# Taking GpSimd's arithmetic out of a fused attention and two-MoE kernel

## The chip, the cores and the metric

The kernel runs on one core of a Trainium2 chip. A core has four compute engines that run side by side: TensorE (PE, the matrix engine), VectorE (DVE), ScalarE (ACT) and GpSimd (POOL). A fifth, SyncE (SP), issues most of the DMAs. The metric is the device time of one execution in microseconds, the median of several runs.

## The reference, cut to what matters

```python
scores = scale * q @ k^T                      # 2 batches, 12 heads, 448 x 448, head size 64
scores = where(upper triangle, -1e9, scores)
attn = exp(scores - max(scores)); attn = attn / (sum(attn) + 1e-9)
x = attn @ v                                  # reshaped to 896 tokens x 768
a = x @ w1; b = x @ w2                        # 768 x 1024 each
y = (a * b @ w3) @ w_out                      # 1024 x 1024, 1024 x 768
h = y @ w_in; g = max(h, 0) ** 2              # 768 x 2048
out = g @ w_out2                              # 2048 x 768
```

## The kernel before, in words

The kernel keeps float32 accuracy on TensorE by splitting each operand into two parts: a rounded one ("hi", fp32r) and the remainder ("lo"). A product is then three fast matmuls: hi x hi, hi x lo and lo x hi. ScalarE makes hi by a rounding copy, and VectorE makes lo by the subtraction x - hi. `parts_of` (L442) records these two steps. Large products use Strassen's scheme with seven products per 2 x 2 block, which needs sums and differences of blocks. Most of these are VectorE's too.

The work has three stages. In the first (until about 158 us of the profile), the 12 pairs of heads go through attention, and TensorE's gaps are filled with the product of w3 and w_out (tiles `w`). `scores` (L620) makes two heads' score blocks, `minimum` adds the mask and takes the row extreme on VectorE, `softmax` (L666) has ScalarE's exponentials, VectorE's reciprocals, and then one division (a multiplication by the reciprocal, L689) per block of 112 rows, eight per pair. `transposes` and `attend` follow on TensorE. The second stage computes a, b and their product with the combined weight matrix. The third (from about 312 us) has four groups of the second MoE: for each, `product` makes h, `g_out` (L1004) applies ReLU and the square on ScalarE, `need_block` (L1020) makes the Strassen blocks of g (sums in `fs`, parts in `g`), and `o_step` multiplies them with w_out2, whose parts lie in `ring`. `into_acc` (L1187) adds the results from PSUM into tiles named `g`. Weights come by DMA into `raw` tiles, are put together in `xs`, and are split into `ring`.

The order of the instructions is worked out while the kernel is built, by `Program` (L26). Each `prog.add(engines, run, reads, writes, ...)` records an operation with its cost on each engine that may run it: "T" TensorE, "A" ScalarE, "V" VectorE, "P" GpSimd, "S" DMA. `order` (L60) gives every operation a due time from the TensorE operations that need it, then simulates the engines greedily: at each step the engine that can begin earliest takes the ready operation with the earliest due time. TensorE's operations keep the order in which the program lists them. The order that comes out is the order of each engine's instructions on the chip, where semaphores keep the dependences.

Three things of this planner belong to GpSimd. An operation marked `port=True` (both operands in SBUF) on VectorE can't begin in the plan while one on GpSimd is running, nor the other way round. An operation that VectorE could also run goes to GpSimd only if it would end there before VectorE could begin to come to it, or if it is due more than `SPARE` = 2500 ns later. And 64 operations end up on GpSimd: 27 of the 96 divisions of the softmax, and 37 subtractions, which are parts and differences of blocks of h and g. Beside that GpSimd builds two constants at the start and issues the 12 accumulating DMAs of `w_sums` (L810).

The divisions' and subtractions' alternatives are recorded like this:

```python
        engines = dve(width) | (pool(width) if any_engine else {})
        prog.add(engines, tt(lo, x, lambda: hi().bitcast(F32), ALU.subtract), src + his, los, port=not psum)
```

All two-operand instructions of VectorE and GpSimd recorded through `tt` have line L433 in the profile; ScalarE's copies have L440.

Of the kernel before, what the change touches and what calls it, by code (L numbers as in the profile page):

```python
# [16 lines left out]
class Op:  # L17
# [4 lines left out]
    def __init__(self, place, engines, run, after, behind, port):  # L22
        self.place, self.engines, self.run, self.port = place, engines, run, port
        self.after, self.behind = after, behind
        self.due = self.start = self.end = None


class Program:
# [4 lines left out]
    SPARE = 2500  # L33
# [4 lines left out]
    def add(self, engines, run, reads=(), writes=(), port=False, after=(), behind=(), turn=None):  # L38
# [11 lines left out]
        op = Op(len(self.ops), engines, run, list(after), [o for o in behind if o not in after], port)  # L50
        if turn:
            self.turns[turn] = op
        for r in reads:
            self.read.setdefault(r, []).append(op)
        for r in writes:
            self.wrote[r], self.read[r] = op, []
        self.ops.append(op)
        return op

    def order(self):  # L60
# [68 lines left out]
def attention_moe_moe2(ctx: ExitStack, tc: tile.TileContext, qk, v, w1, w2, w3, w_out, w_in2, w_out2, out):  # L129
# [210 lines left out]
    engine_of = {"A": nc.scalar, "V": nc.vector, "P": nc.gpsimd}  # L340
# [8 lines left out]

    def pool(width):  # L350
        gap = 110 + 2.28 * width
        return {"P": (gap, gap + 30)}
# [89 lines left out]
    def parts_of(hi, lo, x, width, src, his, los, psum=False, any_engine=False, of=None):  # L442
# [6 lines left out]
    def block_parts(of, n, k, x, src, psum=False, any_engine=False):  # L449
        slot = slot_of_block(of, n, k)  # L450
        parts_of(lambda: part_of_slot(slot, 0), lambda: part_of_slot(slot, 1), x, S, src,
                 part_names(slot, 0), part_names(slot, 1), psum, any_engine, of)
# [29 lines left out]
    def float32(key, words, width, y, names):  # L482
# [16 lines left out]
        prog.add(dve(width, fast=True), lower, [low], [low], port=True)  # L499
        prog.add(dve(width), join, [low, *names], names, port=True)  # L500
# [14 lines left out]
    def w_row(key):  # L515
# [26 lines left out]
        prog.add(dve(width), tt(lo, y, lambda: hi_of(key).bitcast(F32), ALU.subtract), src + his, los, port=True)  # L542
# [77 lines left out]
    def scores(p):  # L620
# [9 lines left out]
        for g in BLOCKS:  # L630
            o = 0
            for i in g:
# [13 lines left out]
                prog.add({"T": (1.856 * w, 1.856 * w + 250)}, run, [("qk", p % 3)],  # L646
# [19 lines left out]
    def softmax(p, j):  # L666
# [169 lines left out]
    for k in range(KH):  # L836
        i, b = slot_in("T2", k), slot_in("B21", k)
        prog.add(dve(S), tt(fs_at(i), fs_at(b), fs_at(i), ALU.subtract), [("fs", i), ("fs", b)], [("fs", i)], port=True)
# [14 lines left out]
    def half_sum(out, x, z, what):  # L853
# [5 lines left out]
        prog.add(dve(HN), tt(half(out), half(x), half(z), what), [xs_half(*x), xs_half(*z)], [xs_half(*out)], port=True)  # L859
# [32 lines left out]
    def need_unit(u):  # L892
# [25 lines left out]
        else:  # L918
# [5 lines left out]
                 src + [("ring", i, "h") for i in slots], [("ring", i, "l") for i in slots], port=True)  # L924
# [19 lines left out]
    def ab_out(nm, m, b, n, i_bank):  # L944
# [12 lines left out]
        else:  # L957
            prog.add(dve(S), negated(row, fs_at(n), fs_at(a), ALU.mult), [("fs", n), ("fs", a)], names, port=True)
# [21 lines left out]
    def ab_sums(d):  # L980

        (r0, n0), (r1, n1), (r2, n2), (r3, n3) = (ab_row(d, i) for i in range(4))
        prog.add(dve(S), tt(r0, r0, r1, ALU.subtract), n0 + n1, n0, port=True)
        prog.add(dve(S), tt(r1, r3, r1, ALU.subtract), n1 + n3, n1, port=True)

        def t2():
            t = take_fs()
            prog.add(dve(S), negated(fs_at(t), r3, r0, ALU.subtract), n3 + n0, [("fs", t)], port=True)
            block_parts("ab", "T2", d, fs_at(t), ("fs", t))
            prog.add(dve(S), negated(r2, r2, fs_at(t), ALU.subtract), [*n2, ("fs", t)], n2, port=True)  # L990
# [13 lines left out]
    def g_out(nm, m, b, n, i):  # L1004
# [10 lines left out]
        parts_of(*part, lambda: fs[:, n, BN:], REST, ("fs", n), his, los, any_engine=True)  # L1015
# [4 lines left out]
    def need_block(g, n, d):  # L1020
# [7 lines left out]
        def sub(out, x, y):  # L1028
            prog.add(dve(BN) | pool(BN), tt(fs_at(out, BN), fs_at(x, BN), fs_at(y, BN), ALU.subtract),
                     [("fs", x), ("fs", y)], [("fs", out)], port=True)  # L1030
# [6 lines left out]
        elif n == "7":  # L1037
# [3 lines left out]
                 his, los, any_engine=True)  # L1041
# [101 lines left out]
    def h_out(n, k, st, i):  # L1143
        o, src = bank_at(i), ("bank", i)

        def block(name, at):
            block_parts("h", name, k, fs_at(at), ("fs", at), any_engine=True)
# [4 lines left out]
        def sub(out, x, y):  # L1152
            prog.add(dve(S), tt(fs_at(out), fs_at(x), fs_at(y), ALU.subtract), [("fs", x), ("fs", y)], [("fs", out)],
                     port=True)
# [183 lines left out]
```

## Time and profile before

| | us |
|---|---|
| median of 3 runs | 534.0 |
| lowest and highest | 533.85 and 537.04 |
| the profiled execution | 534.52 |
| its span, first to last instruction | 532.7 |

The profile comes from that one execution. It gives each engine's busy time, groups of equal instructions with their mean duration, the instructions in order of time, and the chain of waits followed back from the last instruction. Instructions of one engine overlap at their ends, so n in a row take less than n times the duration of one.

### The profile page before, as it was taken

The numbers are of one execution on the slowest core, as the hardware profiler recorded it, in microseconds if no ns is written. First come the engines' busy times: TensorE is split into PE (matmuls) and PEld (weight loads), VectorE is DVE, ScalarE is ACT, GpSimd is POOL, SyncE is SP. The second block draws the span as 40 slices with busy tenths as digits, with TensorE's granted clock in tenths as the row PEclk, the third lists the DMA queues.
The fourth block names the chain that finished last, engine by engine and source line by source line (L and its number), as shares of the span: only waits on it lengthen the run. The fifth ranks groups of instructions, "written<-read, shape, count | busy, mean of one in ns | idle before, by whom it ended". The sixth has DMA issues, their size and how long they took to land.

```text
span 532.7 us, 8568 instructions
## 1 busy us (share of the span) xinstructions
PE 519.2 (97%) x2905; PEld 460.8 (86%) x2905; DVE 492.3 (92%) x1093; ACT 383.9 (72%) x890; POOL 103.2 (19%) x84
## 2 busy tenths in 40 slices
PE   7899999999999999999999999999999999999996
PEld 4658878888879999999999999999999989998985
DVE  5999898898999999997975899999999999999996
ACT  6998887777869565648475577986896489649950
POOL 2222211122110010221100034010115021505050
PEclk9999999999999999999999999999999999999999
DMA  8956554452642469999652402405430454035114
GB/s 317 322 166 220 169 180 148 147 170 61 249 156 83 177 184 252 260 254 248 153 163 93 172 0 73 165 1 201 155 120 0 148 178 150 0 132 175 51 59 149
DMA packets 26572, 81.30 MB, mean 153 GB/s; under 512 B 2400, under 2 KB 13408, under 8 KB 26528
## 3 DMA queue, kind: packets, MB, share of 16 engines
q1 hardware_dynamic: 22752, 75.24, 41.4%
q0 software_dynamic: 3776, 5.51, 6.4%
q8 instruction: 23, 0.38, 0.3%
q14 instruction: 21, 0.17, 0.1%
HBM read 74.84 MB, written 14.55 MB: 168 GB/s over the span
## 4 chain that ended last, share of the span: by engine, by line
PE 54%; DVE 21%; ACT 7%; DMA 2%; issue 2%; DVEq 0%
PE bank L176 43%; DVE g L433 6%; DVE ring L433 5%; PE w L176 5%; DVE xs L433 2%; DVE xs L495 2%; PE pp L704 2%; PE x L176 2%; DVE fs L433 2%; PE s L176 2%; ACT ring L440 1%; DMA raw_w<-in_w 1%; DMA raw_wout<-in_w_out 1%; ACT fs L1010 1%; ACT fs L1011 1%
## 5 line engine op out<-in xcount | busy, mean ns | idle before, releaser
L440 ACT CAST ring<-xs 128x384 fp32r<-128x384 f32 (+1 forms) x194 | 102.3, 542 | 59.2 <-DVE xs L433 21.4
L176 PE MATMUL bank<-xT,ring 128*128 128x448 f32 x630 | 132.2, 366 | 0.0
L433 DVE TENSOR_TENSOR ring<-xs,ring 128x384 fp32r<-128x384 f32 (+1 forms) x194 | 118.9, 631 | 12.2 <-ACT ring L440 12.0
L176 PEld LDWEIGHTS bank<-xT,ring 128*128 128x128 f32 x630 | 117.8, 188 | 9.6 <-ACT bank L440 0.5
L176 PE MATMUL bank<-ring,g 128*128 128x384 f32 x600 | 107.7, 337 | 3.0 <-DVE ring L433 2.0
L176 PEld LDWEIGHTS bank<-ring,g 128*128 128x128 f32 x600 | 103.8, 188 | 6.5 <-DVE ring L433 3.3
L176 PE MATMUL bank<-xB,ring 128*128 128x448 f32 x489 | 103.5, 367 | 0.7 <-ACT ring L440 0.4
L176 PEld LDWEIGHTS bank<-xB,ring 128*128 128x128 f32 x489 | 91.3, 188 | 10.0 <-ACT ring L440 1.4
L433 POOL TENSOR_TENSOR g<-fs,g 128x384 fp32r<-128x384 f32 (+1 forms) x24 | 37.2, 1562 | 127.7 <-ACT g L440 112.5
L672 ACT ACTIVATE p<-p,st 112x448 f32<-112x448 f32 (+3 forms) x96 | 49.9, 533 | 12.1 <-DVE st L662 12.1
L689 POOL TENSOR_SCALAR p<-p,st 112x224 f32<-112x224 f32 (+3 forms) x27 | 33.5, 1244 | 114.3 <-DVE st L681 62.4
L433 DVE TENSOR_TENSOR xs<-xs 128x384 f32<-128x384 f32 x96 | 54.4, 581 | 0.1
L662 DVE CUSTOM_DVE_ANT_0 p<-s,mask 112x224 f32<-112x224 f32 (+3 forms) x96 | 36.7, 440 | 6.4 <-PE s L176 6.3
L440 ACT CAST g<-fs 128x384 fp32r<-128x384 f32 (+1 forms) x88 | 34.4, 413 | 5.2 <-DVE fs L433 4.9
L176 PE MATMUL w<-hl_wout,w 128*128 128x384 f32 x192 | 36.2, 340 | 0.3 <-DVE wraw L433 0.2
L487 ACT ACTIVATE xs<-raw_w 128x768 f32<-128x768 f32 (+1 forms) x30 | 24.3, 814 | 14.7 <-DVE w L433 6.5
L176 PEld LDWEIGHTS w<-hl_wout,w 128*128 128x128 f32 x192 | 32.9, 188 | 1.9 <-issue 0.9
L821 POOL DMA_DIRECT2D s_dram<-w_dram x12 | 13.9, 1184 | 99.6 <-DMA s_dram<-w_dram 99.6
L176 PE MATMUL s<-qk 64*112 64x448 f32 (+3 forms) x192 | 28.2, 439 | 3.9 <-DMA qk<-in_qk 3.9
L433 DVE TENSOR_TENSOR g<-bank,g 128x384 f32<-128x384 f32 x60 | 30.1, 544 | 1.6 <-PE bank L176 1.6
L440 ACT COPY fs<-bank 128x448 f32<-128x448 f32 x49 | 25.8, 527 | 7.6 <-PE bank L176 7.6
L176 PE MATMUL bank<-ab,ring 128*128 128x448 f32 x144 | 29.5, 365 | 0.0
(82 smaller groups left out, 746.7 us busy)
## 6 DMA issues: line engine op xcount, KB each, us to landing
raw_wout<-in_w_out SPq DMA_DIRECT2D x24, 768.0 KB, 4.5
raw_w<-in_w SPq DMA_DIRECT2D x16, 768.0 KB, 4.5
raw_win<-in_w_in SPq DMA_DIRECT2D x16, 768.0 KB, 4.5
raw_w<-in_w SPq DMA_DIRECT2D x16, 512.0 KB, 4.1
qk<-in_qk SPq DMA_DIRECT2D x12, 448.0 KB, 5.7
s_dram<-w_dram POOLq DMA_DIRECT2D x8, 576.0 KB, 9.8
w_dram<-wraw SPq DMA_DIRECT2D x8, 384.0 KB, 2.9
s_dram<-w_dram SPq DMA_DIRECT2D x4, 768.0 KB, 7.1
```

Source lines behind the costliest of these rows:

```text
L176: return nc.tensor.matmul(o, l, r, start=start, stop=stop, **more)
L433: return lambda e: engine_of[e].tensor_tensor(out(), x(), y(), op=what)
L440: return lambda e: engine_of[e].copy(out(), x()) if e == "A" else engine_of[e].tensor_copy(out(), x())
L487: nc.scalar.activation(y(), raws[key][:, :, 1].bitcast(F32), AF.Prelu, scale=2.0 ** -112, alpha=-2.0 ** 32)
L495: nc.vector.scalar_tensor_tensor(yi, yi, 3, raws.pop(key)[:, :, 0], op0=ALU.logical_shift_left, op1=ALU.bitwise_or)
L662: prog.add({"V": (gap, gap + 160)}, lambda e: nc.vector.tensor_tensor_reduce(block(p, j, i), s_t[p, j, g][:CP, o:o + w], mask[:, S - w:], ...
L672: prog.add({"A": (gap, gap + 100)}, lambda e, i=i: nc.scalar.activation(block(p, j, i), block(p, j, i), AF.Exp, bias=st_t[p][:, 0, j, i:i ...
L689: lambda e, i=i: engine_of[e].tensor_scalar(block(p, j, i), block(p, j, i), st_t[p][:, 3, j, i:i + 1], None, ALU.mult),
L704: nc.tensor.transpose(x[0][:CP, o * CP:(o + 1) * CP], block(p, j, i)[:, c * CP:(c + 1) * CP], ident[:CP, :CP])
L821: prog.add({"P": (900, 5000)}, lambda e, x=x, n0=n0, n1=n1: nc.gpsimd.dma_start(out=s_dram[d][:, n0:n1], in_=spread(x, n1 - n0), accum_op= ...
L1010: prog.add(act(S, src[0] == "bank"), lambda e: nc.scalar.activation(r(), x(), AF.Relu), [src], [("fs", n)])
L1011: prog.add(act(S), lambda e: nc.scalar.activation(r(), r(), AF.Square), [("fs", n)], [("fs", n)])
```

## The change

No operation has GpSimd as an alternative any more: the divisions are VectorE's alone, and so are all subtractions. With that, the planner loses its rule for the shared port (the `port` marks and the time that the port is held) and the rule with `SPARE`. One cost of the plan changes too: the scores of the first pair of heads (p == 0) are planned at 3.3 ns per column in place of 1.856. The DMA issues of `w_sums` and the two constants stay with GpSimd.

```diff
-    SPARE = 2500
...
-        port, at_step = 0, 0
+        at_step = 0
...
                 def begin(o):
-                    held = port if e in "PV" and o.port else 0
-                    return max(clock[e], avail[o], held)
+                    return max(clock[e], avail[o])
...
-                if e in "AP":
+                if e == "A":
...
-                        return t0 + o.engines[e][0] < on_v or e == "P" and o.due > t0 + self.SPARE
+                        return t0 + o.engines[e][0] < on_v
...
-            if e in "PV" and o.port:
-                port = t0 + gap
...
-    engine_of = {"A": nc.scalar, "V": nc.vector, "P": nc.gpsimd}
+    engine_of = {"A": nc.scalar, "V": nc.vector}
...
-    def pool(width):
-        gap = 110 + 2.28 * width
-        return {"P": (gap, gap + 30)}
...
-        engines = dve(width) | (pool(width) if any_engine else {})
-        prog.add(engines, tt(lo, x, lambda: hi().bitcast(F32), ALU.subtract), src + his, los, port=not psum)
+        prog.add(dve(width), tt(lo, x, lambda: hi().bitcast(F32), ALU.subtract), src + his, los)
...
-                prog.add({"T": (1.856 * w, 1.856 * w + 250)}, run, [("qk", p % 3)],
+                prog.add({"T": ((3.3 if p == 0 else 1.856) * w, (3.3 if p == 0 else 1.856) * w + 250)}, run, [("qk", p % 3)],
...
-                on_v, on_p = 70 + 0.67 * w, 265 + 2.5 * w
-                prog.add({"V": (on_v, on_v + 85), "P": (on_p, on_p + 30)},
-                         lambda e, i=i: engine_of[e].tensor_scalar(
+                on_v = 70 + 0.67 * w
+                prog.add({"V": (on_v, on_v + 85)},
+                         lambda e, i=i: nc.vector.tensor_scalar(
...
-            prog.add(dve(BN) | pool(BN), tt(fs_at(out, BN), fs_at(x, BN), fs_at(y, BN), ALU.subtract),
-                     [("fs", x), ("fs", y)], [("fs", out)], port=True)
+            prog.add(dve(BN), tt(fs_at(out, BN), fs_at(x, BN), fs_at(y, BN), ALU.subtract),
+                     [("fs", x), ("fs", y)], [("fs", out)])
```

## Rows read from the trace of the kernel before

**Rows 1.** The page: busy us, share of the span, instructions of each engine.
```profile
PE 519.2 (97%) x2905; PEld 460.8 (86%) x2905; DVE 492.3 (92%) x1093; ACT 383.9 (72%) x890; POOL 103.2 (19%) x84
```
**Rows 2.** Stretches of the span: PE, PEld, DVE, ACT, POOL busy us, clock, DMA.
```profile
0.00:158.00 158.00, 152.01 (x1020) 118.55 (x1022) 142.00 (x440) 124.28 (x344) 35.14 (x35) 1.00 0.57 194
...
378.00:479.00 101.00, 99.11 (x527) 93.10 (x526) 100.29 (x194) 72.97 (x164) 23.14 (x18) 1.00 0.33 111
479.00:505.00 26.00, 25.83 (x130) 23.68 (x131) 25.81 (x56) 24.46 (x58) 7.24 (x1) 1.00 0.35 119
505.00:523.00 18.00, 16.39 (x89) 14.90 (x87) 18.00 (x31) 9.00 (x21) 8.17 (x7) 1.00 0.14 44
```
**Rows 3.** The chain that ended last, in order of time: start, us, what.
```profile
158.75 184.03 PE bank L176 x911
...
511.18 1.29 DVE fs L433
```
**Rows 4.** TensorE: two undisturbed runs by time; then its groups, 378.6 to 522 us.
```profile
299.67 13.34 PE L176 MATMUL bank<-ab,ring 128*128 128x448 f32 x65
...
499.73 15.79 PE L176 MATMUL bank<-ring,g 128*128 128x384 f32 x90
...
L176 PE MATMUL bank<-ring,g 128*128 128x384 f32 x413 | 74.4, 337 | 2.9 <-DVE ring L433 2.0 <-ACT ring L440 0.6 <-DVE g L433 0.3
L176 PE MATMUL bank<-xT,ring 128*128 128x448 f32 x180 | 38.6, 367 | 0.0
L176 PE MATMUL bank<-xB,ring 128*128 128x448 f32 x134 | 29.4, 370 | 0.7 <-ACT ring L440 0.4
```
**Rows 5.** GpSimd's groups from 378 us; its DMA issues in the whole run.
```profile
L433 POOL TENSOR_TENSOR g<-fs,g 128x384 fp32r<-128x384 f32 x15 | 23.2, 1559 | 63.0 <-ACT g L440 47.8 <-DVE g L433 15.2
L433 POOL TENSOR_TENSOR fs<-fs 128x384 f32<-128x384 f32 x7 | 10.1, 1446 | 18.4 <-DVE fs L433 18.4
L433 POOL TENSOR_TENSOR g<-fs,g 128x64 fp32r<-128x64 f32 x4 | 5.5, 1381 | 41.0 <-ACT g L440 41.0
...
L821 POOL DMA_DIRECT2D s_dram<-w_dram x12 | 13.9, 1184 | 99.6 <-DMA s_dram<-w_dram 99.6
```
**Rows 6.** VectorE and GpSimd in order of time, 507 to 514 us.
```profile
507.34 1.48 DVE L433 TENSOR_TENSOR g<-bank,g 128x384 f32<-128x384 f32 x3
507.46 4.58 POOL L433 TENSOR_TENSOR g<-fs,g 128x384 fp32r<-128x384 f32 x4 [15.19 <-DVE g L433]
...
508.73 2.44 DVE L433 TENSOR_TENSOR ring<-xs,ring 128x384 fp32r<-128x384 f32 x2
...
511.10 1.36 DVE L433 TENSOR_TENSOR fs<-fs 128x384 f32<-128x384 f32 x1
...
512.01 2.61 POOL L433 TENSOR_TENSOR fs<-fs 128x384 f32<-128x384 f32 x2
```
**Rows 7.** VectorE: ns min/median/max of two groups; then its groups from 378 us.
```profile
L433 DVE TENSOR_TENSOR xs<-xs x96: 540/547/1369, 152.1 to 521.1; 128x384 f32<-128x384 f32 x96
...
L433 DVE TENSOR_TENSOR g<-fs,g x64: 209/544/1039, 333.3 to 524.4; 128x384 fp32r<-128x384 f32 x38, 128x64 fp32r<-128x64 f32 x26
...
L433 DVE TENSOR_TENSOR ring<-xs,ring 128x384 fp32r<-128x384 f32 x78 | 46.5, 620 | 0.0
...
L433 DVE TENSOR_TENSOR xs<-xs 128x384 f32<-128x384 f32 x40 | 24.7, 628 | 0.0
...
L433 DVE TENSOR_TENSOR fs<-fs 128x384 f32<-128x384 f32 x17 | 10.9, 644 | 0.0
...
L433 DVE TENSOR_TENSOR g<-fs,g 128x64 fp32r<-128x64 f32 x20 | 5.0, 259 | 0.4 <-ACT g L440 0.2
```
**Rows 8.** The divisions: GpSimd's group, one of VectorE's by time, TensorE's wait.
```profile
L689 POOL TENSOR_SCALAR p<-p,st 112x224 f32<-112x224 f32 (+3 forms) x27 | 33.5, 1244 | 114.3 <-DVE st L681 62.4
...
120.87 0.45 DVE L689 TENSOR_SCALAR p<-p,st 112x448 f32<-112x448 f32 x1
...
PE pp L704 <- DVE p L689: 0.9, 1, 0.9
```

More of the change, by code (lines that the diff above doesn't have):

```diff
@@ L17, with __init__ @@
 class Op:
-    def __init__(self, place, engines, run, after, behind, port):
-        self.place, self.engines, self.run, self.port = place, engines, run, port
+    def __init__(self, place, engines, run, after, behind):
+        self.place, self.engines, self.run = place, engines, run
         self.after, self.behind = after, behind
@@ L32, with add @@
     HOP = 80
-    SPARE = 2500
     def __init__(self, clock):
         self.ops, self.wrote, self.read, self.clock, self.turns = [], {}, {}, clock, {}
-    def add(self, engines, run, reads=(), writes=(), port=False, after=(), behind=(), turn=None):
+    def add(self, engines, run, reads=(), writes=(), after=(), behind=(), turn=None):
         after, behind = dict.fromkeys(after), dict.fromkeys(behind)
@@ L49, in add @@
             behind[self.turns[turn]] = None
-        op = Op(len(self.ops), engines, run, list(after), [o for o in behind if o not in after], port)
+        op = Op(len(self.ops), engines, run, list(after), [o for o in behind if o not in after])
         if turn:
@@ L498, in float32 @@
         prog.add(act(width, strided=True), prelu, [high], names)
-        prog.add(dve(width, fast=True), lower, [low], [low], port=True)
-        prog.add(dve(width), join, [low, *names], names, port=True)
+        prog.add(dve(width, fast=True), lower, [low], [low])
+        prog.add(dve(width), join, [low, *names], names)
     w3t, w_rows = {}, {}
@@ L541, in w_row @@
         prog.add(act(width), copy(hi, y), src, his)
-        prog.add(dve(width), tt(lo, y, lambda: hi_of(key).bitcast(F32), ALU.subtract), src + his, los, port=True)
+        prog.add(dve(width), tt(lo, y, lambda: hi_of(key).bitcast(F32), ALU.subtract), src + his, los)
         w_rows[key] = names
@@ L837, in attention_moe_moe2 @@
         i, b = slot_in("T2", k), slot_in("B21", k)
-        prog.add(dve(S), tt(fs_at(i), fs_at(b), fs_at(i), ALU.subtract), [("fs", i), ("fs", b)], [("fs", i)], port=True)
+        prog.add(dve(S), tt(fs_at(i), fs_at(b), fs_at(i), ALU.subtract), [("fs", i), ("fs", b)], [("fs", i)])
         give_fs(b)
@@ L857, in half @@
             return lambda: in_slot(of[0])[:, of[1] * HN:(of[1] + 1) * HN]
-        prog.add(dve(HN), tt(half(out), half(x), half(z), what), [xs_half(*x), xs_half(*z)], [xs_half(*out)], port=True)
+        prog.add(dve(HN), tt(half(out), half(x), half(z), what), [xs_half(*x), xs_half(*z)], [xs_half(*out)])
     def need_item(it):
@@ L923, in need_unit @@
         prog.add(dve(width), tt(lambda: t[1], x, lambda: t[0].bitcast(F32), ALU.subtract),
-                 src + [("ring", i, "h") for i in slots], [("ring", i, "l") for i in slots], port=True)
+                 src + [("ring", i, "h") for i in slots], [("ring", i, "l") for i in slots])
     def ring_names(u):
@@ L957, in ab_out @@
         else:
-            prog.add(dve(S), negated(row, fs_at(n), fs_at(a), ALU.mult), [("fs", n), ("fs", a)], names, port=True)
+            prog.add(dve(S), negated(row, fs_at(n), fs_at(a), ALU.mult), [("fs", n), ("fs", a)], names)
             give_fs(n)
@@ L982, in ab_sums @@
         (r0, n0), (r1, n1), (r2, n2), (r3, n3) = (ab_row(d, i) for i in range(4))
-        prog.add(dve(S), tt(r0, r0, r1, ALU.subtract), n0 + n1, n0, port=True)
-        prog.add(dve(S), tt(r1, r3, r1, ALU.subtract), n1 + n3, n1, port=True)
+        prog.add(dve(S), tt(r0, r0, r1, ALU.subtract), n0 + n1, n0)
+        prog.add(dve(S), tt(r1, r3, r1, ALU.subtract), n1 + n3, n1)
         def t2():
             t = take_fs()
-            prog.add(dve(S), negated(fs_at(t), r3, r0, ALU.subtract), n3 + n0, [("fs", t)], port=True)
+            prog.add(dve(S), negated(fs_at(t), r3, r0, ALU.subtract), n3 + n0, [("fs", t)])
             block_parts("ab", "T2", d, fs_at(t), ("fs", t))
-            prog.add(dve(S), negated(r2, r2, fs_at(t), ALU.subtract), [*n2, ("fs", t)], n2, port=True)
+            prog.add(dve(S), negated(r2, r2, fs_at(t), ALU.subtract), [*n2, ("fs", t)], n2)
             give_fs(t)
@@ L1014, in g_out @@
         part = [lambda r=r: g_at("g", at + r * 2 * REST, 1, REST)[:, 0] for r in range(2)]
-        parts_of(*part, lambda: fs[:, n, BN:], REST, ("fs", n), his, los, any_engine=True)
+        parts_of(*part, lambda: fs[:, n, BN:], REST, ("fs", n), his, los)
         g_rows[m, b] = n
@@ L1040, in need_block @@
         parts_of(lambda: g_at("g", at, 2, BN)[:, 0], lambda: g_at("g", at, 2, BN)[:, 1], fs_at(row, BN), BN, ("fs", row),
-                 his, los, any_engine=True)
+                 his, los)
         if n == "6":
@@ L1146, in block @@
         def block(name, at):
-            block_parts("h", name, k, fs_at(at), ("fs", at), any_engine=True)
+            block_parts("h", name, k, fs_at(at), ("fs", at))
         def add(at):
@@ L1152, in sub @@
         def sub(out, x, y):
-            prog.add(dve(S), tt(fs_at(out), fs_at(x), fs_at(y), ALU.subtract), [("fs", x), ("fs", y)], [("fs", out)],
-                     port=True)
+            prog.add(dve(S), tt(fs_at(out), fs_at(x), fs_at(y), ALU.subtract), [("fs", x), ("fs", y)], [("fs", out)])
         if n == "1":
```

6 lines of the change are left out of this document (3 added, 3 removed).

## The prediction

> **What bounds the kernel now.** I read the page's busy line first [rows 1]. TensorE is busy for 519.2 of 532.7 us, VectorE for 492.3, GpSimd for 103.2, so on the average TensorE is the limit. An average over stages hides what matters here: the work that GpSimd gives up goes to VectorE, so the question is in which stages VectorE has room. The stage table answers it [rows 2]. In attention (0 to 158 us) VectorE is busy 142.00 of 158 us; in the three parts of the last stage it is busy 100.29 of 101, 25.81 of 26 and 18.00 of 18 us. Next the chain that ended last [rows 3]: from 158.75 us it is one unbroken run of 911 matmuls (184.03 us), but at 511 us its pieces are VectorE's subtractions.
>
> Then I measured what TensorE loses in that last stage. 65 matmuls of 448 columns take 13.34 us, so a step is (13.34 - 0.37) / 64 = 0.2027 us; 90 of 384 columns take 15.79 us, a step of (15.79 - 0.34) / 89 = 0.1736 us [rows 4]. From 378.6 to 522 us there are 413 of 384 and 180 + 134 = 314 of 448 columns: 413 x 0.1736 + 314 x 0.2027 = 135.3 us in 143.4 us. So about 8 us of TensorE's time is lost there. It is the only large reserve, and it is lost to a saturated VectorE.
>
> **What GpSimd's work costs and returns in the last stage.** From 378 us on GpSimd runs 15 subtractions into g of 384 columns, 7 into fs of 384 and 4 of 64 columns [rows 5]. On VectorE three back-to-back instructions of 384 columns take 1.48 us [rows 6] and the median of one alone is 0.547 us [rows 7], so each occupies (1.48 - 0.547) / 2 = 0.467 us and overlaps the next by 0.08 us. One of 64 columns lasts at least 0.209 us [rows 7]; less that overlap it occupies 0.13 us. Added to VectorE: 22 x 0.467 + 4 x 0.13 = 10.8 us.
>
> Against that stands what GpSimd now takes from VectorE. While GpSimd works at 507.46 to 514.6 us, two ring subtractions take 2.44 us together in place of 0.547 + 0.467 = 1.01, and a subtraction in fs takes 1.36 us in place of 0.547, as do the two behind it. Three subtractions that read one operand from a PSUM bank take 1.48 us beside the same GpSimd work, the normal time [rows 6]. So GpSimd holds up instructions with both operands in SBUF, and only those. In the last stage the means of the 384-column forms are 0.620, 0.628 and 0.644 us, against that median of 0.547, and the excess sums to 78 x 0.073 + 40 x 0.081 + 17 x 0.097 = 10.6 us [rows 7]. The 64-column ones add 20 x (0.259 - 0.217) = 0.8 us (0.217 is my estimate of their undisturbed mean, between the least, 0.209, and the row's mean). Together 11.4 us of VectorE's time are stalls.
>
> So removing GpSimd's work returns 11.4 us and adds 10.8 us: VectorE gets 0.6 us lighter in the last stage. Ends of this term: all stalls stay (+10.8 us), or the stalls go and the added work falls only into gaps (-8 us, all that TensorE loses there, since beyond that TensorE is the bound). I take -0.6, because the slow rows stand exactly beside GpSimd's and the PSUM rows beside them are not slow. In the end stretch from 505 to 523 us the balance is best: 5 g and 2 fs subtractions add 7 x 0.467 = 3.3 us, while the slow pieces read above return 2.44 - 1.01 + 3 x 0.81 = 3.9 us [rows 6]. Those 0.6 us are the whole of the term, so in the rest of the stage the balance is about zero: there GpSimd ran beside PSUM reads more often, and cost nothing.
>
> The Trainium skill, SBUF - State Buffer, section "Who interferes with whom", says that such a pair of instructions excludes each other for a whole instruction. By that, 22 GpSimd subtractions at their spacing of 4.58 / 4 = 1.15 us could hold VectorE for 25 us, and the change would return 25 - 10.8 = 14 us, more than TensorE can lose. The rows show 0.82 us per hit, and none beside a PSUM operand (the page excepts that case too), so the sum goes by the rows.
>
> **Attention.** 27 of 96 divisions move [rows 8]. The widest form (448 columns) takes 0.45 us at 120.87 us, where GpSimd does nothing; less the overlap of 0.08 us it occupies 0.37 us. That is at most 27 x 0.37 = 10 us, and likely about 7, since most of those moved are narrower. VectorE has 16 us of idle time there [rows 2], so even with nothing returned it fits in the sum. TensorE, meanwhile, waited for a division just once, for 0.9 us [rows 8]. I expect a third of that wait to go, -0.3 us (ends: -0.9 to +1, one or two new waits of that size). What is late next is the copy out of PSUM behind the transposes, which is ScalarE's and unchanged.
>
> **158 to 378 us.** 3 subtractions into g and 1 into fs of 384 columns, 2 of 64 and 5 of 448 move. TensorE is the bound in that stage, and the chain passes through it alone for 184 us [rows 3]; the work adds 4 x 0.467 + 2 x 0.13 + 5 x 0.535 = 4.8 us to VectorE (0.535: my estimate for 448 columns, 0.467 and 64 more columns at the 0.33 / 320 us per column between the two widths). I did not weigh what returns, because TensorE covers it. Term: 0. If that cover failed and nothing returned, the cost would be those 4.8 us.
>
> **The planner.** It no longer keeps VectorE and GpSimd from running at the same time. Since the sequence of TensorE is fixed by the program, only the order on VectorE and ScalarE moves. The dearer first scores (3.3 in place of 1.856 ns per column, 1120 columns: 1.6 us) shift the planned times of everything behind; no instruction is added. Term 0, with 1 us to either side. GpSimd's 12 DMA issues stay; each waited for the DMA before it [rows 5], not for arithmetic, so emptying the queue brings nothing.
>
> **Sum.** -0.6 - 0.3 = -0.9 us. The profiled execution took 534.52 us (span 532.7 and 1.8 around it) and would take 533.6; the median of the runs is 534.0, 0.5 lower, which gives 533.1. A measurement of this kernel tells about 1% (5.3 us) from no change.
>
> **Rivals.**
> 1. *TensorE gets its lost time back.* The stalls hit ring subtractions that TensorE waits for, and the GpSimd work was for later; with accurate plan times the urgent instruction always comes first. All 8 us back gives 526; over 1% needs 5.3 of the 8. For it: TensorE's named waits after 378 us are mostly for ring [rows 4]. Against: VectorE is busy 144.1 of 145 us there (the three parts together) [rows 2], and an engine that is always busy gains only by having less to do, which is 0.6 us.
> 2. *VectorE becomes too heavy (slower).* In the last stage the added 10.8 us come in full, but the stalls go only partly, because some of the long subtractions waited for something else than GpSimd, or because GpSimd's time beside PSUM reads was free and the new order has no such free time. With no stall returned: 534.0 + 10.8 = 545 us. It decides once less than half of the 11.4 us returns (10.8 - 5.5 = 5.3 us). The Trainium skill, Perfetto Trace Analysis, section "Optimizing Scalar/DVE Operations", speaks for this rival: a saturated VectorE is where it would offload, if with a caution about the port. For it also: VectorE has no idle time to hide anything [rows 2]. Against: the slow rows coincide with GpSimd's [rows 6].
> 3. *The new order is merely unlucky or lucky*, with ScalarE the late one in the stretch 479 to 505 us, where it is busy 24.46 of 26 us [rows 2]: plus or minus 3 us, 531 to 536. It is within 1%.
>
> **How the numbers follow.** The forecast with rival 3 inside it: 0.77; rival 1 beyond 1%: 0.12; rival 2 beyond 1%: 0.11. The range takes the likeliest case whole (531 to 536 us, with rival 3) and goes on towards the first two until about 2 in 10 are left out: to 528.5 us, where TensorE has back 5.5 of its 8 us, and to 538.0 us, where about 5 of the 11.4 us of stalls have stayed and the rest has gone.
>
> **What would show it.** In the profile after: VectorE with about 1093 + 64 = 1157 instructions (27 divisions, 37 subtractions) at a busy time within 3 us of 492; the means of the 384-column ring, xs and fs subtractions back at 0.547 us, with none above 0.65; GpSimd left with its 12 DMA issues and the set-up; VectorE still busy over 98% from 378 to 523 us, and the end chain still its subtractions. Rival 1 would show fewer than 3 us lost by TensorE after 378 us; rival 2 the same long subtractions without GpSimd, or TensorE's waits for ring and g grown. I am wrong if VectorE's load in that stage moves by more than 3 us, or if the time moves with the load unchanged.

## The result, and the profile after

| | before | after |
|---|---|---|
| median of 5 runs, us | 534.57 | 529.6 |
| lowest and highest | 533.85 and 537.04 | 529.0 and 530.35 |
| ratio, 95% interval | | 0.989 [0.9857, 0.9922] |
| the profiled execution | 534.52 | 529.73 |
| its span | 532.7 | 528.0 |

The change takes 5.0 us (0.8 to 1.4%) off. The forecast was 533.1 us with a range of 528.5 to 538.0. The time lies inside the range, near its fast end, and the gain is more than five times the forecast 0.9 us.

First the page's busy line, and then the stage table, of the kernel after (columns as in [rows 1] and [rows 2]).

```profile
PE 514.4 (97%) x2905; PEld 461.2 (87%) x2905; DVE 490.8 (93%) x1157; ACT 385.4 (73%) x890; POOL 15.2 (3%) x20
```

```profile
0.00:158.00 158.00, 151.31 (x1034) 120.01 (x1035) 143.44 (x470) 126.02 (x346) 1.62 (x8) 1.00 0.58 195
...
378.00:479.00 101.00, 99.74 (x534) 94.52 (x533) 100.71 (x213) 74.76 (x165) 0.00 (x0) 1.00 0.36 121
479.00:505.00 26.00, 25.94 (x136) 24.40 (x135) 26.00 (x59) 24.72 (x59) 0.00 (x0) 1.00 0.20 74
505.00:523.00 18.00, 17.36 (x99) 16.68 (x97) 18.00 (x40) 5.80 (x13) 0.00 (x0) 1.00 0.28 88
```

VectorE has taken 64 instructions more (1157 for 1093) and its busy time is still 1.5 us lower (490.8 for 492.3 in [rows 1]). In the last three stretches it is busy 144.71 of 145 us, where it was 144.10 [rows 2]. That it was and is always busy there was read rightly. But TensorE does more in the same stretches: 534 + 136 + 99 = 769 matmuls for 527 + 130 + 89 = 746.

VectorE's groups from 378 to 523 us, after (columns as in [rows 7]):

```profile
L425 DVE TENSOR_TENSOR ring<-xs,ring 128x384 fp32r<-128x384 f32 x76 | 40.3, 550 | 0.0
...
L425 DVE TENSOR_TENSOR xs<-xs 128x384 f32<-128x384 f32 x40 | 21.6, 551 | 0.0
L425 DVE TENSOR_TENSOR fs<-fs 128x384 f32<-128x384 f32 x24 | 13.2, 551 | 0.0
...
L425 DVE TENSOR_TENSOR g<-fs,g 128x64 fp32r<-128x64 f32 x24 | 4.9, 217 | 0.0
```

The means of 0.620, 0.628 and 0.644 us are 0.550 and 0.551 now; the 64-column one is 0.217. Every stall of [rows 7] is gone, so all of it was GpSimd's.

Where the 4.7 us of the span (532.7 to 528.0) come from is read from the times at which TensorE starts its pieces. First the kernel after, TensorE in order of time: the transposes of one pair, the first product matmul behind attention, the first on the parts of g, and the last 15 matmuls.

```profile
77.28 2.08 PE L695 MATMUL pp<-ident,p 112*112 112x112 f32 x20
...
157.04 0.47 PE L172 MATMUL bank<-xB,ring 128*128 128x448 f32 x1
...
388.85 26.63 PE L172 MATMUL bank<-ring,g 128*128 128x384 f32 x150
...
519.62 2.90 PE L172 MATMUL bank<-ring,g 128*128 128x384 f32 x15 [0.16 <-DVE g L425]
```

The same places in the kernel before:

```profile
77.53 2.91 PE L704 MATMUL pp<-ident,p 112*112 112x112 f32 x20
...
158.69 0.47 PE L176 MATMUL bank<-xB,ring 128*128 128x448 f32 x1
...
390.92 21.14 PE L176 MATMUL bank<-ring,g 128*128 128x384 f32 x118
...
521.23 7.72 PE L176 MATMUL bank<-ring,g 128*128 128x384 f32 x41 [0.72 <-DVE ring L433]
```

The stretch from the first matmul on the parts of g to the last matmul holds 711 matmuls in both. Its line in the table of stretches, after:

```profile
388.85:522.52 133.67, 132.19 (x711) 125.55 (x709) 133.67 (x285) 95.93 (x214) 0.00 (x0) 1.00 0.29 97
522.52:528.00 5.48, 0.00 (x0) 0.00 (x0) 0.76 (x2) 0.00 (x0) 0.00 (x0) 0.98 0.67 232
```

and before:

```profile
390.92:528.95 138.03, 134.33 (x711) 125.23 (x709) 136.10 (x263) 95.84 (x216) 36.30 (x24) 1.00 0.30 101
```

| part of the span | before | after | difference |
|---|---|---|---|
| start to the first product (attention) | 158.69 | 157.04 | -1.65 |
| from there to the first matmul on the parts of g | 232.23 | 231.81 | -0.42 |
| from there to the last matmul (last stage) | 138.03 | 133.67 | -4.36 |
| from there to the end of the span | 3.75 | 5.48 | +1.73 |

So the last stage gives 4.4 us, attention 1.7, and the end takes 1.7 back. In the last stage VectorE was busy for 136.10 us and idle for 1.93; now it is busy for 133.67 and never idle. By the paces of [rows 4] TensorE needs 450 x 0.1736 + 253 x 0.2027 = 129.4 us there, about 130 with eight short matmuls, so it lost 8 us before and loses somewhat under 4 now.

Where VectorE's idle time lay is read from its last subtraction and its last additions, before:

```profile
524.37 0.54 DVE L433 TENSOR_TENSOR g<-fs,g 128x384 fp32r<-128x384 f32 x1
...
527.94 1.60 DVE L433 TENSOR_TENSOR g<-bank,g 128x384 f32<-128x384 f32 x3 [1.63 <-PE bank L176]
```

and after:

```profile
519.94 0.55 DVE L425 TENSOR_TENSOR g<-fs,g 128x384 fp32r<-128x384 f32 x1
520.41 2.88 DVE L425 TENSOR_TENSOR g<-bank,g 128x384 f32<-128x384 f32 x6
```

Of the 1.93 us, 1.63 are one wait for the last matmuls, when VectorE had no subtraction left to do. Only 0.30 us lay before. The last stage and the end are therefore better cut at the end of that last subtraction. VectorE came to it 133.99 us after the first matmul on the parts of g and comes to it in 131.64 us now, 2.35 us sooner. From there to the end of the span the kernel took 7.79 us and takes 7.51. TensorE's last matmul falls 4.04 us behind the subtraction before and 2.03 after, since 41 matmuls stood behind TensorE's last wait and now 15 do. But the additions and stores that follow VectorE's last subtraction take nearly as long as before, so 1.7 of these 2.0 us come back at the end. Of the 2.35 us, 0.30 are idle time, about 0.6 are two subtractions that now run before the stage begins (one into ring, one of 64 columns), and the remaining 1.45 are stalls less added work.

The chain that ended last, after:

```profile
157.11 262.49 PE bank L172 x1339
...
519.10 3.73 DVE g L425 x8
```

TensorE is the chain for 262 us without a break, where it was 184 in [rows 3], and the end is VectorE's still.

### The profile page after: what moved, and what is told of

The parts are those of the page before. It is cut to its first block, busy times and chain, and to the rows that moved or that the text cites. A ratio compares the mean times of both kernels' runs of the same rounds, so it can differ in the third digit from the quotient of the medians.

```text
span 528.0 us, 8458 instructions
## 1 busy us (share of the span) xinstructions
PE 514.4 (97%) x2905; PEld 461.2 (87%) x2905; DVE 490.8 (93%) x1157; ACT 385.4 (73%) x890; POOL 15.2 (3%) x20
## 4 chain that ended last, share of the span: by engine, by line
PE 72%; DVE 19%; ACT 5%; DMA 2%; issue 1%; DVEq 0%
PE bank L172 51%; PE w L172 11%; DVE g L425 6%; PE s L172 4%; PE x L172 3%; PE pp L695 3%; DVE ring L425 3%; DVE fs L425 2%; DVE xs L486 2%; ACT ring L432 2%; DVE p L653 2%; DVE xs L425 1%; DMA raw_w<-in_w 1%; ACT xs L478 1%; DVE p L680 1%
## 5 line engine op out<-in xcount | busy, mean ns | idle before, releaser
L425 DVE TENSOR_TENSOR ring<-xs,ring 128x384 fp32r<-128x384 f32 (+1 forms) x194 | 111.4, 588 | 12.1 <-ACT ring L432 11.8
L172 PE MATMUL bank<-ring,g 128*128 128x384 f32 x600 | 106.1, 336 | 1.3 <-DVE g L425 1.3
L663 ACT ACTIVATE p<-p,st 112x224 f32<-112x224 f32 (+3 forms) x96 | 50.1, 536 | 10.1 <-DVE st L653 10.1
L425 DVE TENSOR_TENSOR xs<-xs 128x384 f32<-128x384 f32 x96 | 51.7, 551 | 0.1
L425 DVE TENSOR_TENSOR g<-fs,g 128x384 fp32r<-128x384 f32 (+1 forms) x88 | 36.7, 430 | 0.0
L425 DVE TENSOR_TENSOR g<-bank,g 128x384 f32<-128x384 f32 x60 | 31.5, 551 | 0.0
L680 DVE TENSOR_SCALAR p<-p,st 112x448 f32<-112x448 f32 (+1 forms) x96 | 29.1, 360 | 0.1
L172 PEld LDWEIGHTS bank<-ab,ring 128*128 128x128 f32 x144 | 27.0, 188 | 2.1
```

What stands on the lines that cost most here:

```text
L172: return nc.tensor.matmul(o, l, r, start=start, stop=stop, **more)
L425: return lambda e: engine_of[e].tensor_tensor(out(), x(), y(), op=what)
L663: prog.add({"A": (gap, gap + 100)}, lambda e, i=i: nc.scalar.activation(block(p, j, i), block(p, j, i), AF.Exp, bias=st_t[p][:, 0, j, i:i ...
L680: lambda e, i=i: nc.vector.tensor_scalar(block(p, j, i), block(p, j, i), st_t[p][:, 3, j, i:i + 1], None, ALU.mult),
```

## The experiments

Twelve kernels were run. Each ratio is to runs of the kernel before on the same chip, whose median was between 534.9 and 535.6 us there. At the outset three theories stood against each other: (A) the stalls that GpSimd caused were worth more than the work that came over; (B) the planner makes a better order when it plans only for engines that really run freely; (C) it is the dearer planned cost of the first scores, a change of its own inside this change.

**Is it the planned cost of the first scores? (C)** It is taken back out of the change, and then it is made alone.

```diff
-                prog.add({"T": ((3.3 if p == 0 else 1.856) * w, (3.3 if p == 0 else 1.856) * w + 250)}, run, [("qk", p % 3)],
+                prog.add({"T": (1.856 * w, 1.856 * w + 250)}, run, [("qk", p % 3)],
```

> The changed kernel with one part undone: the scores of the first pair of heads are planned at 1.856 ns per column again, GpSimd still computes nothing. Theory A (the gain of the change, 4.9 us, comes from GpSimd's arithmetic being gone): 529 to 531 us. Rival C (the dearer first scores give a planned start that matches the chip, and that makes attention shorter by the 1.6 us seen in the traces): 531 to 532 us, with TensorE's first product after attention at 158.5 us again in place of 157.0.

Measured: 529.5 us, ratio 0.9902 [0.9873, 0.993]. The first product starts at 156.03 us and the last stage takes 133.49 us. All of the gain is there without the dearer cost.

The second kernel is the kernel before with that one line (the same diff the other way round).

> The kernel before with the other part alone: first scores planned at 3.3 ns per column, GpSimd keeps its share and the planner its port. Theory A: 534 to 535 us, no change. Rival C: 532.5 to 533.5 us, and the first product after attention starts at about 157.0 us.

Measured: 534.33 us, 0.9982 [0.9964, 1.0], at most 0.4 per cent. Its first product starts at 157.79 us, 0.9 us earlier than before, where theory C expected 157.0. C falls.

**The load alone, in the old order (A against B).** This kernel takes the plan of the kernel before, GpSimd's share and the port rule included, and only runs GpSimd's 64 operations on VectorE, each in its place in the order.

```diff
         for o in prog.order():
-            o.run(o.engine)
+            o.run("V" if o.engine == "P" and "V" in o.engines else o.engine)
```

> The order planned for the kernel before, unchanged, but the 64 operations that it gives to GpSimd are issued on VectorE at their places. Theory A (the stalls on the port were what cost; VectorE's load falls by 1 to 3 us whatever the order): 530 to 532.5 us. Rival B (the order counts: a plan that matches the engines puts the urgent instruction first): 533.5 to 537 us, at or above the kernel before, with the 384-column subtractions at 0.55 us all the same and VectorE's busy time within 1 us of the changed kernel's 490.8.

Measured: 534.93 us, 0.9996 [0.9972, 1.002]. Its page has the engines as after, and its stretches show the last stage as long as before:

```profile
PE 519.3 (97%) x2905; PEld 460.6 (86%) x2905; DVE 492.7 (92%) x1157; ACT 384.7 (72%) x890; POOL 15.0 (3%) x20
```

```profile
391.40:529.61 138.21, 134.08 (x711) 125.08 (x709) 135.44 (x286) 95.99 (x216) 0.00 (x0) 1.00 0.30 100
```

GpSimd computes nothing, VectorE runs x1157 without a stall, and nothing is won. The exchange of stalls for work is even, as the prediction had summed it, and A falls. What differs between this kernel and the changed one is nothing but the order, and that is worth 534.93 - 529.6 = 5.3 us (0.9996 against 0.989 in ratios to the kernel before). One part of the expectation missed: VectorE's busy time of 492.7 us is 1.9 above the changed kernel's, not within 1.

VectorE's last subtraction and last additions here:

```profile
525.50 0.57 DVE L433 TENSOR_TENSOR g<-fs,g 128x384 fp32r<-128x384 f32 x1
...
528.61 1.60 DVE L433 TENSOR_TENSOR g<-bank,g 128x384 f32<-128x384 f32 x3 [1.14 <-PE bank L176]
```

VectorE comes to the end of its last subtraction after 134.67 us (133.99 before, 131.64 after). Up to there it is busy for 133.04 us, 0.65 less than before, as the prediction had it, but idle for 1.63 in place of 0.30: it waits for ScalarE's copies (0.9 us in all) and for DMAs (0.7), which it doesn't in the new order. The old order was made for two engines. So a part of the 5.3 us mends waits that the load brings into it. (The profiled execution took 535.82 us, the median 534.93. Its 384-column instructions last 0.560 us in place of 0.551, but back to back they start 0.47 us apart in both.)

**Which part of the change brings the better order?** The divisions alone leave GpSimd, planned anew; then the subtractions alone.

```diff
-                prog.add({"V": (on_v, on_v + 85), "P": (on_p, on_p + 30)},
+                prog.add({"V": (on_v, on_v + 85)},
```

> The kernel before with one part of the change: all 96 divisions of the softmax are VectorE's, planned anew; the 37 subtractions and the port rule stay. Theory B2 (what GpSimd's work costs beyond its stalls is an order that the chip can't follow, in each stage by itself): attention ends 1.5 to 2 us earlier, 532.5 to 534 us. Theory A2 (the gain comes from the last stage alone): 534.5 to 535.5 us.

Measured: 533.39 us, 0.9965 [0.9938, 0.9993], or -1.9 us. The stretches by time, first product and last stage:

```profile
156.26 0.47 PE L176 MATMUL bank<-xB,ring 128*128 128x448 f32 x1
```

```profile
388.44:526.87 138.43, 134.36 (x711) 125.16 (x709) 136.46 (x264) 96.39 (x217) 42.02 (x24) 1.00 0.30 100
```

Attention is 2.4 us shorter (156.26 for 158.69), the last stage as before, and 41 matmuls stand behind TensorE's last wait.

```diff
-        engines = dve(width) | (pool(width) if any_engine else {})
+        engines = dve(width)
...
-            prog.add(dve(BN) | pool(BN), tt(fs_at(out, BN), fs_at(x, BN), fs_at(y, BN), ALU.subtract),
+            prog.add(dve(BN), tt(fs_at(out, BN), fs_at(x, BN), fs_at(y, BN), ALU.subtract),
```

> The other part: all 37 subtractions are VectorE's, planned anew; 27 divisions may stay with GpSimd, with the port rule. Theory B2: 531 to 532.5 us, the larger share, since the loss of TensorE in the last stage is the larger one. Theory A2: 529.5 to 530.5 us, the whole gain.

Measured: 531.13 us, 0.9934 [0.9914, 0.9954], or -3.5 us. Its last stage:

```profile
391.69:525.09 133.40, 131.93 (x711) 125.58 (x709) 133.36 (x285) 95.62 (x213) 0.00 (x0) 1.00 0.29 96
```

Here the last stage is as short as after (133.40 us, VectorE idle for 0.04), 15 matmuls stand behind TensorE's last wait, and attention is little better than before (157.97 us to the first product; the transposes that took 2.91 us still do). The two parts act in a stage each, and 1.9 + 3.5 = 5.4 us is the whole gain within the intervals.

**Is the order bad because the plan has GpSimd's costs wrong?** The planner holds a 384-column subtraction of GpSimd at 110 + 2.28 x 384 = 0.99 us, where [rows 5] has means of 1.4 to 1.6. This kernel is the one before with higher costs. Those of the divisions come near the rows (at 448 columns 600 + 2.7 x 448 = 1.81 us, where the trace of before has a mean of 1.79). Those of the subtractions go only part of the way: 1.32 us for 384 columns, and 0.31 us for 64, which [rows 5] has at 1.38.

```diff
-        gap = 110 + 2.28 * width
+        gap = 110 + 3.15 * width
...
-                on_v, on_p = 70 + 0.67 * w, 265 + 2.5 * w
+                on_v, on_p = 70 + 0.67 * w, 600 + 2.7 * w
```

> The kernel before, with only the plan's costs of GpSimd raised to what the trace shows beside a busy VectorE (a 384-column subtraction 1.32 us in place of 0.99, a 224-column division 1.20 us in place of 0.83). GpSimd and the port rule stay. Theory B2 (the old order was made for a GpSimd faster than the real one, and a truer plan mends it): 530 to 532.5 us. Rival B3 (GpSimd's work is no gain on this chip however it is planned, since each piece holds the port): 533.5 to 536 us.

Measured: 533.75 us, 0.9977 [0.9958, 0.9996], or -1.2 us. The first product starts at 155.67 us, so attention gains 3.0 us. The last stage gets longer:

```profile
388.19:527.77 139.58, 134.20 (x711) 125.52 (x709) 137.33 (x263) 95.12 (x215) 35.98 (x24) 1.00 0.31 101
```

The time lies in the range of B3 and not in that of B2. Higher costs mend attention while GpSimd still works there; they don't mend the last stage, where VectorE is loaded as before and idle for 2.25 us (1.63 of it the wait behind its last subtraction). So the wrong cost can explain the first part of the gain. For the second it is not the answer as far as this kernel goes; subtractions planned at their full measured cost were not tried.

**What the port rule was worth.** The kernel before, with GpSimd, but without the rule that keeps the two engines apart in the plan.

```diff
-                    held = port if e in "PV" and o.port else 0
+                    held = 0
```

> The kernel before with GpSimd at work but without the port in the plan: both engines may be planned at the same time. Theory A: GpSimd gets more work and each piece stalls VectorE unplanned, so slower than before, 536 to 541 us. If the rule for the port in the plan only cost time (it held VectorE back without need): 530 to 533 us.

Measured: 551.85 us, 1.0308 [1.0279, 1.0336]. That is 17 us slower, more than either theory had. The page:

```profile
PE 524.5 (95%) x2905; PEld 465.9 (85%) x2905; DVE 503.4 (92%) x1060; ACT 386.6 (70%) x890; POOL 133.2 (24%) x117
```

Without the rule the plan sees GpSimd as free help and sends it 97 operations (x117, less 20 others) in place of 64; VectorE has 33 instructions fewer than before and is busy for 11 us more (503.4 for 492.3): its instructions take longer. Over the whole run the 176 ring subtractions of 384 columns have a mean of 0.641 us where before they have 0.596. TensorE, kept waiting, lost clock as well: its granted clock was 0.66 from 320 to 330 us, after it had been busy for 7.48 of the 10 us before, and 0.83 from 480 to 490, after 8.32 of 10. So not all of the 17 us is VectorE's. The rule is thus not idle, but what it allows is a draw at best.

**The stall by itself.** The changed kernel, with GpSimd given work that no one needs, on a spare tile, from 395.5 us on: 1 + 24 subtractions of 384 columns that read SBUF; then 1 subtraction and 48 memsets of the same tile, which only write.

```diff
+        if (g, tile, n) == (1, 0, 0):
+            prog.add({"P": (1000, 1030)}, lambda e: nc.gpsimd.tensor_tensor(spare, a(), a(), op=ALU.subtract), dst, [("spare",)])
+            for _ in range(24):
+                prog.add({"P": (1000, 1030)}, lambda e: nc.gpsimd.tensor_tensor(spare, spare, spare, op=ALU.subtract), [("spare",)], [("spare",)])
```

> The changed kernel, plus one GpSimd subtraction that reads a finished tile of the second group and 24 more on a spare tile of 384 columns that nothing else uses. No engine waits for them. If a GpSimd instruction that reads SBUF holds up VectorE's subtractions with both operands in SBUF: these take 1.2 to 1.4 us in place of 0.55 for the about 25 to 32 us from 395 us on, those with a PSUM operand stay at 0.55, and with about 0.5 us lost per piece the kernel takes 537 to 545 us. If the long subtractions of before had another cause: 529 to 531 us.

> The same with 48 GpSimd fills of the spare tile (they write and read nothing) in place of the 24 subtractions, about the same time in all. If only GpSimd's reads hold up VectorE's subtractions: 529 to 531 us, all subtractions at 0.55 us. If any GpSimd work does: 535 to 545 us as with the reads.

Measured: 542.53 us with the subtractions (1.0134 [1.0119, 1.0149]) and 530.17 with the memsets (0.9908 [0.9887, 0.9928]). The second is the changed kernel's time. The first, in order of time:

```profile
397.12 26.13 POOL L1191 TENSOR_TENSOR spare<-spare 128x384 f32<-128x384 f32 x24
...
397.21 1.16 DVE L427 TENSOR_TENSOR ring<-xs,ring 128x384 fp32r<-128x384 f32 x1
398.29 1.18 DVE L427 TENSOR_TENSOR g<-fs,g 128x384 fp32r<-128x384 f32 x1
399.39 1.18 DVE L427 TENSOR_TENSOR ring<-xs,ring 128x384 fp32r<-128x384 f32 x1
...
404.89 1.01 DVE L427 TENSOR_TENSOR g<-bank,g 128x384 f32<-128x384 f32 x2
...
418.80 1.18 DVE L484 TENSOR_SCALAR raw_win<-raw_win 128x768 uint32<-128x768 uint32 x1
...
427.73 0.55 DVE L484 TENSOR_SCALAR raw_win<-raw_win 128x768 uint32<-128x768 uint32 x1
```

The second, at the same place:

```profile
397.13 24.22 POOL L1191 MEMSET spare<- 128x384 f32 x48
...
397.24 0.55 DVE L427 TENSOR_TENSOR ring<-xs,ring 128x384 fp32r<-128x384 f32 x1
```

Beside reads of GpSimd's, VectorE's subtractions start 1.10 us apart in place of 0.467; beside its writes they are undisturbed, and so are those with a PSUM operand (two in 1.01 us). Both kernels have the first of GpSimd's subtractions, so they differ by 24 of them. VectorE has 1157 instructions in both and is busy for 502.1 us beside the subtractions and 490.6 beside the memsets: 11.5 / 24 = 0.48 us for each. VectorE does the same subtraction in 0.467. That is the even exchange of the load-alone kernel, in one number. In the kernel's time it is (542.53 - 530.17) / 24 = 0.52 us, and this holds a second effect. TensorE, kept waiting (busy for 7.03 us from 410 to 420), was granted 0.66 of its clock from 420 to 430 us, and 0.50 (1.2 of 2.4 GHz) between 422 and 427 (columns as in [rows 2]):

```profile
420.00:430.00 10.00, 8.24 (x31) 7.57 (x32) 10.00 (x17) 4.17 (x8) 3.10 (x3) 0.66 0.45 157
```

The Trainium skill, SBUF - State Buffer, section "Who interferes with whom", says that a VectorE instruction with two SBUF inputs contends with a GpSimd instruction that reads SBUF, and not with one that only writes it, and the memsets agree with it. Of VectorE's two-port performance mode it says that the engine that issues first blocks the other for the whole instruction. For these subtractions the rows show less: one of each fits into a step of 1.10 us (GpSimd's 24 take 26.13 us, 1.09 each). One after the other they would take 0.467 + 1.01 = 1.48 us, with 1.01 us from the shortest of GpSimd's in the kernel before:

```profile
519.76 1.01 POOL L433 TENSOR_TENSOR g<-fs,g 128x384 fp32r<-128x384 f32 x1 [5.13 <-ACT g L440]
```

**Is it the luck of one order?** Any change to a planned cost shuffles the order. Both kernels get another hop between engines in the plan.

```diff
-    HOP = 80
+    HOP = 100
```

> The kernel before with another constant of the plan: 100 ns between engines in place of 80. The work of each engine stays as it is, the order changes in many places. If the 5 us between the two kernels is the luck of one order: anywhere from 529 to 540 us. If an order with GpSimd in it is held up as such: 533 to 537 us.

> The changed kernel with the same constant of the plan, 100 ns in place of 80. If the gain is the luck of one order: anywhere from 527 to 536 us. If an order without GpSimd keeps its gain: 528.5 to 531 us.

Measured: the kernel before 534.37 us (1.0 [0.9983, 1.0018]), the changed one 529.73 (0.992 [0.9897, 0.9943]). Each stays at its own time in another order, 4.6 us apart. Together with the kernel without the dearer first scores (529.5) that is three orders planned without GpSimd within 0.3 us, so the gain is not one lucky order. One mark tells the two plans apart in the runs: 41 matmuls stand behind TensorE's last wait in the orders planned with GpSimd's subtractions (60 in the one without the port rule). In those planned without them it is 15, or TensorE doesn't wait at all in the last 26 us (the changed kernel with the longer hop).

**Can the 1.7 us at the end be had back?** After its last matmul the changed kernel needs 5.48 us. The window from there in the table above has a DMA share of 0.67 at 232 GB/s, and VectorE's last six instructions (520.41 us, above) are additions for the output: they and the stores come last, in a burst. Here what no TensorE operation needs is due earlier.

```diff
         for o in self.ops:
-            o.due = nominal.get(o, t + 3000)
+            o.due = nominal.get(o, t - 6000)
```

> The changed kernel, with the operations that no TensorE operation needs (the last additions and the output's stores) due 6 us before the end of the plan in place of 3 us after it. After the last matmul the changed kernel needs 5.48 us, the kernel before 3.75. Theory T1 (that tail is longer because the output's additions are put last and the stores come in one burst): the tail falls to about 4 us, the last stage stays, and the time is 1 to 1.7 us lower, 528 to 528.6 (ratio to the kernel before near 0.987). Theory T2 (VectorE is full there, so additions put earlier only push the subtractions that TensorE waits for later): the tail falls by as much, but the stretch from the first matmul on the parts of g to the last matmul grows from 133.67 us by 1 us or more, and the time is 529.5 to 531.

Measured: 530.2 us (528.84 to 532.6), 0.991 [0.9883, 0.9936], no faster than the change alone. The stretches of its last stage and end:

```profile
387.77:523.20 135.43, 132.50 (x711) 125.73 (x709) 133.98 (x285) 95.86 (x214) 0.00 (x0) 1.00 0.30 101
523.20:527.00 3.80, 0.00 (x0) 0.00 (x0) 0.59 (x2) 0.00 (x0) 0.00 (x0) 0.99 0.43 155
```

The end falls by 1.68 us, and the last stage grows by 1.76. TensorE's last piece shows where:

```profile
517.06 6.14 PE L172 MATMUL bank<-ring,g 128*128 128x384 f32 x32 [1.71 <-DVE ring L425]
```

TensorE waits 1.71 us for a ring subtraction that now stands behind output additions. Three additions, not six, are left behind VectorE's last subtraction, which ends 132.97 us after the stage's first matmul in place of 131.64; from there to the end of the span it takes 6.26 us in place of 7.51. On a full VectorE the two are the same microseconds, as theory T2 had it.

## Why the prediction was right and wrong

- **The last stage's load: right.** The forecast was that stalls (11.4 us) and added work (10.8 us) nearly cancel. The order-kept kernel gives 0.9996 and a VectorE 0.65 us lighter in the last stage, and the spin pair 0.48 us of VectorE's time for a GpSimd subtraction against 0.467. In the new order VectorE's busy time up to its last subtraction fell by 2.05 us; of this two instructions (x285 for 263 + 24 = 287), about 0.6 us, are only earlier in the run.
- **The means, the counts, the engines: right.** 0.550 and 0.551 us for the 384-column groups, none above 0.65; VectorE x1157; GpSimd with x20, of which 12 are the DMA issues; VectorE busy 144.71 of 145 us; the end chain its subtractions and additions.
- **"The planner. Term 0, with 1 us to either side": wrong, and the step that failed.** The order planned without GpSimd is worth 5.3 us (534.93 to 529.6), the whole gain. The argument was that an always busy engine gains only by having less to do. By that nothing but the load could bring VectorE to its last subtraction sooner. The runs show that with the same load the order alone moves that moment from 134.67 to 131.64 us after the stage's first matmul: 1.63 us of waits for ScalarE and DMAs that the old order has and the new one has not, and 1.40 us of busy time, among it the subtractions that now run before the stage. The prediction's own sign of being wrong, a time that moves with the load unchanged, is what came (VectorE busy 144.71 us for 144.10 from 378 to 523).
- **The range: right by the part added for rival 1.** The likeliest case, 531 to 536 us, does not hold 529.6. The range holds it because it was drawn on to 528.5 for a rival with a chance of 0.12, not by the mechanism that the sum rests on.
- **Rival 1 (TensorE gets its lost time back): partly what happened.** It put the cause where it was, "with accurate plan times the urgent instruction always comes first", with a chance of 0.12. Of the 8 us of TensorE's loss a little over 4 came back, the end took 1.7 of them, and attention added its part. What is left of the loss, 3.7 us, is not under the 3 that was its sign. The row held against it (VectorE busy 144.1 of 145 us) told how full VectorE was, and nothing of the order in it.
- **Rival 3 (lucky or unlucky order, 3 us either way): wrong.** Orders planned alike differ by 0.3 us without GpSimd and by 0.6 with it (534.37 for 534.93, hardly clear of noise); the difference lies between plans with and without GpSimd.
- **Attention, "-0.3": too small.** Measured -1.65 us in the changed kernel and -2.4 with the divisions alone. The prediction looked at waits for divisions, of which there was one. Half of the gain lies elsewhere, in the waits of TensorE's weight loads from 75 to 130 us, before:

```profile
PEld pp L704 <- DVE st L662: 0.8, 3, 0.4
```

  The transposes wait for `minimum` (L662); as I read it, they need a PSUM bank that the scores hold until then. It is late because VectorE runs late there. In order of time, before:

```profile
75.98 0.95 DVE L433 TENSOR_TENSOR hl_wout<-xs,hl_wout 128x768 fp32r<-128x768 f32 x1
76.85 0.61 DVE L662 CUSTOM_DVE_ANT_0 p<-s,mask 112x448 f32<-112x448 f32 x1
```

  and after:

```profile
74.07 0.95 DVE L425 TENSOR_TENSOR hl_wout<-xs,hl_wout 128x768 fp32r<-128x768 f32 x1
74.94 0.62 DVE L653 CUSTOM_DVE_ANT_0 p<-s,mask 112x448 f32<-112x448 f32 x1
```

  The same two instructions come 1.9 us earlier, and the 20 transposes take 2.08 us in place of 2.91, with no such wait left in the view. These 0.8 us don't hang on GpSimd's work: in two kernels planned with it, the one with the dearer first scores alone and the one with the longer hop, the same transposes take 2.08 and 2.13 us, and the first product starts at 157.79 and 157.86. What brings the other 0.8 us was not traced.
- **"GpSimd holds up instructions with both operands in SBUF, and only those": too narrow.** The shift of raw_win has one SBUF operand and took 1.18 us beside GpSimd's reads, 0.55 otherwise. It changed no term.
- **The first scores' cost and 158 to 378 us: right.** Nothing measurable for the first, -0.4 us for the second.

Open is which property of the plan with GpSimd makes VectorE later in the last stage and leaves 41 matmuls behind the last wait. It is not the 64 operations (order kept: no gain). A higher cost for them, still below the measured one, did not mend it (139.58 us there). What remains untried, beside the full cost, is that single GpSimd instructions last very differently: one at 485.03 us took 7.24 us [rows 2, the 479 to 505 row has it alone], which no fixed cost can plan.

## What to carry to other kernels

Where a planner orders the work, a change to which engine does it is two changes, the load and the order: run the new load in the old order before you explain the gain by either. A helper engine that shares a port with the full one is worth what it saves less what it holds up (here 0.467 us against 0.48), and the order planned with it can be worse, which no balance of busy times shows. For an engine that is always busy, ask when it comes to the last thing that others need, and look at where its idle time lies before you count it as a reserve.

## What the runs showed of the hardware

- In a steady contest a VectorE subtraction and a GpSimd subtraction of 384 float32 columns share one step of 1.10 us (VectorE alone 0.467); 24 of GpSimd's kept VectorE busy for 11.5 us longer and cost the kernel 12.4, some of it with TensorE at a granted clock of 0.66.
- GpSimd's memsets of the same tile hold up nothing (0.55 us for VectorE's subtraction beside them), while its subtractions hold up also a one-operand shift on VectorE (1.18 us for 0.55).
- The contest is not always even. In the kernel before, one GpSimd subtraction took 7.24 us in place of 1.01, while VectorE's subtractions beside it kept their pace (four in 1.95 us):

```profile
485.03 7.24 POOL L433 TENSOR_TENSOR g<-fs,g 128x384 fp32r<-128x384 f32 x1 [20.41 <-ACT g L440]
...
485.83 1.95 DVE L433 TENSOR_TENSOR ring<-xs,ring 128x384 fp32r<-128x384 f32 x4
```

- Without the planner's rule, 33 fewer instructions kept VectorE busy 11 us longer, and the kernel took 3.1% more.
